# Two edits to an attention and mixture-of-experts kernel: the order and the queues of the first loads, and the place of one pair of copies

## The chip, the cores and the metric

The kernel runs on one core of a Trainium2 chip. The metric is the device time of one execution in microseconds (us). A core has five engines that run their own instruction streams in order and meet through semaphores: TensorE (PE; its weight loads are listed apart as PEld), VectorE (DVE), ScalarE (ACT), GpSimd (POOL) and SyncE (SP), which here issues nearly all loads and stores.

## The reference

Two layers, of which the second takes the first one's output. All arrays are fp32.

```python
# attention: B, H, S, D = 4, 8, 768, 64; 24 blocks of 32 tokens
mask = |block_i - block_j| <= 1, or either of them is block 0 or 23,
       or block_j is one of the 3 blocks drawn for block_i (sampled_blocks[24, 3])
attn = softmax(where(mask, q @ k.T / 8, -1e9)) @ v
# mixture of experts on x[3072, 512] (attn by token, heads side by side), 8 experts of 512 -> 1024 -> 512
logits = x @ w_gate + modality_bias[modality_id]
e_idx  = argmax(logits);  gate_w = softmax(logits)[e_idx]
out    = gate_w * (relu(x @ w1[e_idx]) @ w2[e_idx])
```

## The kernel before

**Attention.** The batches are worked in two halves of two. For each half, the first and the last block of queries see all keys ("dense" items); the other 22 blocks are taken two at a time, as 11 tiles per half, 22 in all, numbered g = 0 to 21 ("sparse" items). A tile's keys and values are gathered on chip from those it needs: block 0 and 23, the neighbours, and the drawn blocks.

- The dense keys `kd`, queries `qd` and values `vd` are loaded at the start (`dense_k`, `dense_q`, `dense_v`). `dense_k(0)` is three DMAs: the first part of the keys (blocks 0 to 15 and 16 to 23), then the second part.
- `blk_raw` holds the drawn blocks' numbers, sent to all partitions. POOL copies them to `rb_i` (L212, `block_ids`), and DVE makes from them the masks of the sparse tiles in small steps (`tables`, L242 to L287). Engines also read `rb_i` for the addresses of the drawn blocks.
- `share_k` (L465, L469, L481, on POOL) copies a tile's keys out of `kd` into one of two key buffers. `fetch_v` and `fetch_own` (L490 to L496, L520, on SP) load a tile's values from memory into one of two value buffers; `share_v` (L503, on POOL) copies two strips of 32 partitions that the last tile's buffer holds already. `share_v` also loads the numbers of a later tile's blocks into POOL's registers, as long as there are any left.
- A dense item's steps: S scores (L378), M maximum (L391 to L394, DVE), X exponential (L400, ACT), T transposes (L410), A copies (L417), W weighing with the values (L430, L432), O division. A sparse item's: S (L532), M masking and minimum (L540, DVE), X (L548, ACT), T (L557), A (L562), W with the strips that all queries of the tile share (`weigh_shared`, L579), V with the drawn ones (`weigh_own`, L588), O, then the gate (L595 to L608).

**Order.** The order of all instructions on every engine is written by hand. The beginning is the list `START`, in which `blk` is POOL's copy of the block list, `SP16` sixteen steps of DVE's tables, `S00` the first dense scores and `M00` the first maximum:

```python
blk SP16 S00 S01 M00 S02 M01 X00 T00 X01 M02 T01 M03 X02 A00 T02 X03 A01 T03 kl0 ...
```

After it a loop goes through ticks, one item per tick: each step of an item lags its scores by a fixed count (`LAG`), and loads and copies hang on (tick, place) pairs, counted from the last item of an earlier tile. `VS = (11, 7)` puts a tile's `share_v` 11 ticks behind the last item of the tile two before it, at place 7; `VL` and `VG` do the same for `fetch_v` and `fetch_own`. `EARLY = (3, 3)` steps, at place 3, a generator that prepares the first two groups of the experts.

**Experts.** Tokens are routed in groups of 256 rows of one expert. Finished rows go to memory (`x_d`, L1235), and a group's rows are gathered from there by POOL with an indirect DMA, two of 128 rows per group (`gather`, L735). Group 0's gather is issued while attention still runs, as soon as 16 of the 24 row tiles are written. PE turns the rows (`column`, L742), then come the layers: up (L753 to L755), relu, down (L768 to L770), each as three products of high and low parts, which ACT and DVE split (L721, L724); results go out by an indirect DMA (L789).

The program's tiles, DMAs and waits are set by the framework: a DMA of SP or ACT signals one of eight semaphores in turn.

Of the kernel before, what the change touches and what calls it, by code (L numbers as in the profile page):

```python
# [13 lines left out]
I32 = mybir.dt.int32  # L14
# [6 lines left out]
P = 128  # L21
# [18 lines left out]
NM = NB // 2 - 1  # L40
# [27 lines left out]
QP = (-2, 2)  # L68
VL = (8, 1)
VS = (11, 7)  # L70
VG = ((9, 6), (10, 3))

DENSE_IN = ((19, 14, 30), (49, 38, 44))
# [15 lines left out]
def attention_moe(ctx, tc, kD, qD, qH, v0, v1, blocks, modality, w_gate, bias, w1, w2, out):  # L89
    nc = tc.nc  # L90
# [28 lines left out]
    with ExitStack() as actx:  # L119
# [9 lines left out]
        def slot(n, dt=F32):  # L129
            return big.tile([P, 3 * 1024 + 2], dt, name="slot", tag=f"slot{n}", bufs=1)  # L130
# [8 lines left out]
        qd = {}  # L139
# [3 lines left out]
            nc.sync.dma_start(q_raw.rearrange("p n f -> p (n f)"), qH[half, m])  # L143
            return q_raw.rearrange("p n (u q) -> p u n q", q=32)

        def dense_q(half, u0=0, u1=8):
            if half not in qd:
                qd[half] = work.tile([P, HB * NPAIR, 64], F32, name="qd", bufs=1)
            nc.sync.dma_start(qd[half][:, u0:u1].rearrange("p u q -> p (u q)"), qD[half][:, 64 * u0:64 * u1])

        def dense_k(b, cs=(0, 1), js=None):
            if b not in kd:
                kd[b] = slot(KD_SLOT[b])[:, 0:3072].rearrange("p (c j f) -> p c j f", c=2, j=NB)
            for c in cs:
                for j0, j1 in js or (((0, 16), (16, 24)) if (b, c) == (0, 0) else ((0, 24),)):
                    nc.sync.dma_start(kd[b][:, c, j0:j1, :].rearrange("p j f -> p (j f)"), kD[b, :, c, j0 * 64:j1 * 64])
# [5 lines left out]
                nc.sync.dma_start(vd[b][:, t:t + n, :], vH[b // HB][t * P:(t + n) * P, b % HB].rearrange("(t p) f -> p t f", p=P))  # L162

        blk_raw = const.tile([P, NB * 3 * 2], I32, name="blk_raw")
        nc.sync.dma_start(blk_raw, blocks.bitcast(I32).rearrange("a b -> (a b)").partition_broadcast(P))
        dense_q(0, 0, 4)
        wg_raw = const.tile([P, NPAIR, E], F32, name="wg_raw")
        mod_raw = const.tile([P, NT, 2], I32, name="mod_raw")
        b_raw = const.tile([P, 2, E], F32, name="b_raw")

        dense_k(0)
        dense_q(0, 4, 8)
        dense_k(1, (0,))
        dense_v(0)
# [281 lines left out]
        def key_numbers(g):  # L456
            i = 2 * (g % NM) + 1
            picked[g] = nc.values_load_multi_w_load_instructions(
                rb_i[0:1, 3 * i:3 * i + 6], [ET.Pool], min_val=0, max_val=NB - 1, skip_runtime_bounds_check_because=NO_CHECK)[1]

        def share_k(m, half):
            i, g = 2 * m + 1, half * NM + m
            kg = kbuf[g % 2]
            if m:
                nc.gpsimd.tensor_scalar(kg[:, 3:5, :], kbuf[(g - 1) % 2][:, 7:9, :], 1.0, 1.0, ALU.mult, ALU.mult)  # L465

            def put(slots, blocks, bs):
                for b in bs:
                    nc.gpsimd.tensor_scalar(kg[:, slots, b * P:(b + 1) * P].rearrange("p s (c f) -> p c s f", c=2), kd[half * HB + b][:, :, blocks, :], 1.0, 1.0, ALU.mult, ALU.mult)  # L469

            if g not in picked:
                key_numbers(g)
            for bs in ((0,), (1,)) if g == 0 else (range(HB),):
                if m < 2:
                    put(slice(5, 7), slice(0, NB, NB - 1), bs)
                if m == 0:
                    put(slice(3, 5), slice(i - 1, i + 1), bs)
                put(slice(7, 9), slice(i + 1, i + 3), bs)
                for k, reg in enumerate(picked[g]):
                  for b in bs:  # L480
                    nc.gpsimd.tensor_copy(kg[:, k + k // 3 * 6, b * P:(b + 1) * P].rearrange("p (c f) -> p c f", c=2), kd[half * HB + b][:, :, bass.ds(reg, 1), :].rearrange("p c j f -> p c (j f)"))  # L481


        def fetch_v(m, half):
            i, g = 2 * m + 1, half * NM + m
            vg = vbuf[g % 2]
            vrow = vH[half].rearrange("(j s) b f -> s j (b f)", s=BLK)
            if m < 2:
                for n, j in ((0, 0), (1, NB - 1)):
                    nc.sync.dma_start(vg[32 + 32 * n:64 + 32 * n, 1, :], vrow[:, j, :])  # L490
            if m == 0:
                nc.sync.dma_start(vg[0:32, 1:3, :], vrow[:, i:i + 3:2, :])
                nc.sync.dma_start(vg[96:P, 0:2, :], vrow[:, i - 1:i + 2:2, :])
                return
            nc.sync.dma_start(vg[0:32, 2, :], vrow[:, i + 2, :])
            nc.sync.dma_start(vg[96:P, 1, :], vrow[:, i + 1, :])  # L496


        def share_v(m, half):
            g = half * NM + m  # L500
            new, old = vbuf[g % 2], vbuf[(g - 1) % 2]
            for r, c in ((slice(96, P), 0), (slice(0, 32), 1)):
                nc.gpsimd.tensor_scalar(new[r, c, :], old[r, c + 1, :], 1.0, 1.0, ALU.mult, ALU.mult)  # L503
            g = max(picked) + 1
            if g < 2 * NM:
                key_numbers(g)
# [8 lines left out]
        def fetch_own(m, half, n):  # L515
            i, g = 2 * m + 1, half * NM + m
            vg = vbuf[g % 2]
            vrow = vH[half].rearrange("(j s) b f -> s j (b f)", s=BLK)
            for k, reg in enumerate(own[g][3 * n:3 * n + 3]):
                nc.sync.dma_start(vg[32 * (k + n):32 * (k + n) + 32, 2 * n, :], vrow[:, bass.ds(reg, 1), :].rearrange("p j f -> p (j f)"))  # L520
# [676 lines left out]
        def side(t, f, place=7):  # L1197
            work_at.setdefault((t, place), []).append(f)
# [44 lines left out]
        def q_load(m, half):  # L1243
            qraw[m, half] = fetch_q(half, m)
            own_numbers(m, half)

        spares.append(tables())
        side(Q_IN, lambda: dense_q(1))
        for b in (2, 3):
            for t in range(6):  # L1250
# [5 lines left out]
        last = lambda g: at["s", g // NM, g % NM, 1, 1]  # L1256
        for g in range(2 * NM):
            half, m = divmod(g, NM)
            t = at["s", half, m, 0, 0]
            kl = lambda m=m, half=half: q_load(m, half)  # L1260
            qp = lambda m=m, half=half: share_k(m, half)
            vl = lambda m=m, half=half: fetch_v(m, half)
            vg = [lambda m=m, half=half, n=n: fetch_own(m, half, n) for n in range(2)]
            if g < 2:
                loads.update({f"kl{g}": kl, f"qp{g}": qp, f"vl{g}": vl, "vs1": lambda: share_v(1, 0), **{f"v{n}{g}": vg[n] for n in range(2)}})
                continue
            kt = last(g - 2) + KL[0]
            pt = max(kt, t + QP[0])
            vt = last(g - 2) + VL[0]
            side(kt, kl, KL[1])  # L1270
            side(pt, qp, QP[1])
            side(vt, vl, VL[1])
            if m:
                side(last(g - 2) + VS[0], lambda m=m, half=half: share_v(m, half), VS[1])
            for n in range(2):
                side(last(g - 2) + VG[n][0], vg[n], VG[n][1])

# [166 lines left out]
```

## Time and profile before

| what | value |
|---|---|
| median of 3 runs | 535.45 us (535.43 to 536.15) |
| the profiled execution | 536.03 us, span 534.3 us, mean granted PE clock 0.987 |
| PE busy | 514.9 us, 96% of the span |
| PEld, DVE, ACT, POOL busy | 82%, 71%, 63%, 40% |
| DMA | 119.44 MB, mean 224 GB/s |
| idle PE, ended by something | a few waits of at most 2.7 us each |

How to read it: the profiled execution is one run, its span goes from the first to the last instruction, and the device time has 1.7 us more around it. The engines' busy times are shares of that span. A line such as L503 is a line of the kernel's source; the same line stands for all tiles, so that a tile is told by its time. In a timeline, a row has the start, the duration, the engine, the line, the operation, what it writes and reads, and in brackets how long the engine stood idle before and what ended that. "issue" there means a wait for nothing that the profile shows. "SPq" is the queue side of an engine, which issues DMAs. Attention with its routing takes the first 232 us or so, the experts the rest.

### The profile page before, as it was taken

To read this page: it belongs to the slowest core of one execution; us is meant where nothing else is said; L and a number is where in the kernel's file an instruction comes from. 1 tells how busy PE (TensorE), PEld (TensorE's weight loads), DVE (VectorE), ACT (ScalarE), POOL (GpSimd) and SP (SyncE) were. 2 spreads that over 40 slices of the span, in tenths; PEclk is the share of its full clock that TensorE was granted. 3 is DMA by queue.
4 is the path that set the end of the run, shared out by engine and by line. 5 is a ranking of instruction groups with operands and counts; after the bars stand their busy time and mean duration, and the time that the engine had idled before them with its cause. 6 is when DMAs were issued, how large, how long until landed. Compare 5 with 4: busy or idle time off the path is not lost.

```text
span 534.3 us, 19017 instructions
## 1 busy us (share of the span) xinstructions
PE 514.9 (96%) x7298; PEld 436.1 (82%) x7298; DVE 377.2 (71%) x1139; ACT 335.2 (63%) x765; POOL 214.9 (40%) x451
## 2 busy tenths in 40 slices
PE   7999999998999999899999999999999999999995
PEld 5667776766778777788989898998989899898984
DVE  7995698683788999867997656556565655656553
ACT  4689877884988878835456554546555454655552
POOL 3577685574468884323155022030302203030213
PEclk9999999997999999899999999999999999999998
DMA  7995887898846798965888686676758677675840
GB/s 278 339 234 153 238 244 224 243 229 223 232 126 194 198 231 252 274 193 200 238 288 303 227 261 200 237 252 202 244 177 261 203 227 242 213 246 180 257 155 23
DMA packets 49443, 119.44 MB, mean 224 GB/s; under 512 B 7744, under 2 KB 8128, under 8 KB 49344
## 3 DMA queue, kind: packets, MB, share of 16 engines
q1 hardware_dynamic: 45248, 105.02, 64.5%
q0 software_dynamic: 4096, 13.12, 7.3%
q8 instruction: 59, 0.97, 0.8%
q14 instruction: 40, 0.33, 0.2%
HBM read 105.52 MB, written 12.86 MB: 222 GB/s over the span
## 4 chain that ended last, share of the span: by engine, by line
issue 40%; PE 39%; DVE 7%; DMA 6%; POOL 6%; SPq 2%; ACT 1%; POOLq 0%; DVEq 0%; ACTq 0%
PE bank L557 7%; PE bank L532 6%; PE bank L579 4%; PE bank L588 4%; POOL slot L735 3%; DMA out<-slot,si 2%; DMA slot<-kD 2%; PE bank L605 2%; POOL out L789 2%; PE bank L595 2%; DVE y L540 2%; PE bank L753 1%; PE bank L769 1%; PE bank L770 1%; PE bank L768 1%
## 5 line engine op out<-in xcount | busy, mean ns | idle before, releaser
L724 DVE TENSOR_TENSOR slot<-slot 128x1024 fp32r<-128x1024 f32 x99 | 123.1, 1248 | 89.3 <-ACT slot L721 87.5
L721 ACT CAST slot<-slot 128x1024 fp32r<-128x1024 f32 x104 | 108.1, 1048 | 102.1 <-PE bank L754 52.1
L753 PE MATMUL bank<-slot 128*128 128x256 f32 x384 | 108.4, 282 | 0.0
L755 PE MATMUL bank<-slot 128*128 128x256 f32 x384 | 107.8, 281 | 0.0
L754 PE MATMUL bank<-slot 128*128 128x256 f32 x384 | 107.7, 280 | 0.0
L789 POOL DMA_INDIRECT out<-slot,si x20 | 25.4, 1270 | 178.6 <-ACT slot L785 175.6
L548 ACT ACTIVATE a<-y,mn 128x256 f32<-128x256 f32 x176 | 88.7, 511 | 7.7 <-DVE mn L540 7.6
L768 PE MATMUL bank<-slot 128*128 128x512 f32 x192 | 76.6, 399 | 0.0
L769 PE MATMUL bank<-slot 128*128 128x512 f32 x192 | 75.9, 395 | 0.0
L770 PE MATMUL bank<-slot 128*128 128x512 f32 x192 | 75.8, 395 | 0.0
L753 PEld LDWEIGHTS bank<-slot 128*128 128x128 f32 x384 | 72.3, 188 | 0.6
L754 PEld LDWEIGHTS bank<-slot 128*128 128x128 f32 x384 | 72.1, 188 | 0.4
L755 PEld LDWEIGHTS bank<-slot 128*128 128x128 f32 x384 | 72.2, 188 | 0.0
L540 DVE CUSTOM_DVE_ANT_1 y<-bank,smask 128x256 f32<-128x256 f32 x176 | 66.3, 416 | 0.6 <-PE bank L532 0.2
L481 POOL COPY slot<-slot 128x128 f32 x264 | 63.9, 294 | 0.0
L562 ACT COPY at<-bank 128x512 f32<-128x512 f32 x88 | 50.6, 576 | 12.8 <-PE bank L557 12.7
L557 PE MATMUL bank<-ident,a 128*128 128x128 f32 x352 | 52.8, 284 | 0.6 <-ACT a L400 0.5
L503 POOL TENSOR_SCALAR slot<-slot 32x1024 f32<-32x1024 f32 x40 | 41.9, 1048 | 28.0 <-PE bank L588 10.2
L532 PE MATMUL bank<-slot,q_raw 64*32 64x256 f32 x1408 | 48.8, 382 | 1.1 <-DMA q_raw<-qH 0.7
L770 PEld LDWEIGHTS bank<-slot 128*128 128x128 f32 x192 | 36.1, 188 | 8.4
L557 PEld LDWEIGHTS bank<-ident,a 128*128 128x128 f32 x352 | 38.9, 142 | 4.7 <-ACT a L548 0.8
L769 PEld LDWEIGHTS bank<-slot 128*128 128x128 f32 x192 | 36.1, 188 | 7.8 <-DVE slot L724 0.4
(302 smaller groups left out, 855.4 us busy)
## 6 DMA issues: line engine op xcount, KB each, us to landing
slot<-w SPq DMA_DIRECT2D x100, 512.0 KB, 4.0
slot<-v SPq DMA_DIRECT2D x180, 128.0 KB, 4.0
x_d<-xr SPq DMA_DIRECT2D x22, 256.5 KB, 5.3
q_raw<-qH SPq DMA_DIRECT2D x22, 256.0 KB, 4.8
slot<-v SPq DMA_DIRECT2D x16, 256.0 KB, 4.9
slot<-kD SPq DMA_DIRECT2D x13, 256.0 KB, 4.2
slot<-v SPq DMA_DIRECT2D x4, 768.0 KB, 11.9
slot<-w SPq DMA_DIRECT2D x10, 256.0 KB, 5.1
```

Source lines behind the costliest of these rows:

```text
L532: nc.tensor.matmul(sp[u][32 * pr:32 * pr + 32, b * 256:(b + 1) * 256], lhsT=q[r, b * NPAIR + pr, n, :], rhs=kv[r, s0:s0 + 8, b, pr, :], st ...
L540: nc.vector.tensor_tensor_reduce(y[:, u, :].rearrange("p (s f) -> p s f", s=8), sp[u][:, b * 256:(b + 1) * 256].rearrange("p (s f) -> p s ...
L548: nc.scalar.activation(a[:, u, :], y[:, u, :], AF.Exp, bias=mn[:, u:u + 1], scale=-1.0, accum_out=total[:, u:u + 1])
L557: nc.tensor.transpose(tp[:, k:k + P], a[:, u, c * P:(c + 1) * P], ident)
L721: nc.scalar.copy(h, s)
L724: (eng or (nc.gpsimd if n in POOL_SPLITS else nc.vector)).tensor_tensor(l, s, h.bitcast(F32), ALU.subtract)
L753: nc.tensor.matmul(o, lhsT=h[:, fs], rhs=xh[g % 2][:, c, :], start=c == 0 and f % 2 == 0, stop=False)
L754: nc.tensor.matmul(o, lhsT=h[:, fs], rhs=xl[g % 2][:, c, :], start=False, stop=False)
L755: nc.tensor.matmul(o, lhsT=l[:, fs], rhs=xh[g % 2][:, c, :], start=False, stop=c == 3 and f % 2 == 1)
L768: nc.tensor.matmul(o, lhsT=hh[0][:, f, ts_], rhs=h[:, fs], start=f == 0, stop=False)
L769: nc.tensor.matmul(o, lhsT=hh[0][:, f, ts_], rhs=l[:, fs], start=False, stop=False)
L770: nc.tensor.matmul(o, lhsT=hl[f // 4][:, f % 4, ts_], rhs=h[:, fs], start=False, stop=f == 7)
```

## The change

Two edits.

1. The first loads. Before, SP issued in this order: block list, first half of the queries, the keys of batch 0 (three DMAs), second half of the queries, and so on. After, SP begins with the first two DMAs of the keys; the first half of the queries and then the block list are issued by ACT, ahead of its first instruction; SP goes on with the keys' second part and the rest as before. `dense_q` takes the issuing engine as an argument.
2. The copies of `share_v` for g = 20, the last tile but one, move from 11 to 8 ticks behind the last item of tile 18, at the same place 7. In POOL's order they now stand ahead of the two indirect DMAs of group 0's gather (L735) instead of behind them. All other tiles keep their place.

```diff
 VS = (11, 7)
+VS_SOON = (8, 7)
...
-        def dense_q(half, u0=0, u1=8):
+        def dense_q(half, u0=0, u1=8, eng=nc.sync):
             if half not in qd:
                 qd[half] = work.tile([P, HB * NPAIR, 64], F32, name="qd", bufs=1)
-            nc.sync.dma_start(qd[half][:, u0:u1].rearrange("p u q -> p (u q)"), qD[half][:, 64 * u0:64 * u1])
+            eng.dma_start(qd[half][:, u0:u1].rearrange("p u q -> p (u q)"), qD[half][:, 64 * u0:64 * u1])
...
         blk_raw = const.tile([P, NB * 3 * 2], I32, name="blk_raw")
-        nc.sync.dma_start(blk_raw, blocks.bitcast(I32).rearrange("a b -> (a b)").partition_broadcast(P))
-        dense_q(0, 0, 4)
...
-        dense_k(0)
+        dense_q(0, 0, 4, nc.scalar)
+        dense_k(0, (0,))
+        nc.scalar.dma_start(blk_raw, blocks.bitcast(I32).rearrange("a b -> (a b)").partition_broadcast(P))
+        dense_k(0, (1,))
         dense_q(0, 4, 8)
         dense_k(1, (0,))
         dense_v(0)
...
             if m:
-                side(last(g - 2) + VS[0], lambda m=m, half=half: share_v(m, half), VS[1])
+                vs = VS_SOON if g == 2 * NM - 2 else VS
+                side(last(g - 2) + vs[0], lambda m=m, half=half: share_v(m, half), vs[1])
```

## The prediction

> **What bounds the kernel now.** I read the page first (busy shares), then busy time by stretch, then the waits of TensorE (PE), then the timeline at the two places that the change touches.
>
> ```profile
> PE 514.9 (96%) x7298; PEld 436.1 (82%) x7298; DVE 377.2 (71%) x1139; ACT 335.2 (63%) x765; POOL 214.9 (40%) x451
> 6.00:24.00 18.00, 15.18 (x224) 9.69 (x229) 16.48 (x59) 10.59 (x33) 7.55 (x25) 1.00 1.01 361
> 24.00:38.00 14.00, 13.49 (x306) 9.64 (x294) 13.22 (x59) 11.35 (x39) 10.60 (x32) 1.00 0.94 228
> 38.00:205.00 167.00, 160.71 (x4137) 124.26 (x4136) 128.43 (x611) 137.90 (x449) 116.15 (x321) 0.98 0.77 214
> ```
>
> The page's row gives shares of the span, the others one stretch each: length, busy time of PE, PEld, DVE, ACT, POOL, then granted clock, DMA share, GB/s. From 24 us on PE is busy all but 0.5 us of 14 and 6.3 of 167: a microsecond lost or won ahead of 24 goes through to the end. Before 24 PE idles 2.8 us while DVE has 16.48 of 18 and DMA is full. So part one of the change (the first loads) is judged by what DVE and DMA do before 24 us, part two (the copies of tile 20, the last but one) by what PE waits for around 216 us.
>
> **Part one, the start.** The timeline (start, duration, engine, line, what ended the idle time), then from the waits of DVE between 4 and 25 us the one that is not in the timeline above it, and from the list of DMA issues the size and the time from issue to landing:
>
> ```profile
> 0.81 0.40 SPq L165 DMA_DIRECT2D blk_raw<-blocks  x1
> 0.81 1.28 ACT L214 ACT_TABLE_LOAD   x1 [0.81 <-PEq L1437]
> 1.26 0.42 SPq L149 DMA_DIRECT2D qd<-qD  x1
> 1.73 1.37 SPq L156 DMA_DIRECT2D slot<-kD  x3
> 3.99 0.24 POOL L212 COPY rb_i<-blk_raw 128x72 int32<-128x72 int32 x1 [1.99 <-DMA blk_raw<-blocks]
> 4.26 0.20 DVE L242 CAST rb<-rb_i 128x72 f32<-128x72 int32 x1 [0.43 <-POOL rb_i L212]
> 6.88 0.41 PEld L378 LDWEIGHTS bank<-slot,qd 64*64 64x64 f32 x8 [0.45 <-DMA slot<-kD]
> 7.85 0.19 DVE L268 TENSOR_TENSOR rm<-rm,t 128x24 f32<-128x24 f32 x1
> 7.96 0.69 DVE L391 TENSOR_REDUCE nm<-bank 128x1 f32<-128x512 f32 x1
> 9.10 1.52 PE L378 MATMUL bank<-slot,qd 64*64 64x512 f32 x16 [1.35 <-DMA slot<-kD]
> 9.32 0.69 ACT L400 ACTIVATE a<-bank,nb__263 128x512 f32<-128x512 f32 x1 [7.02 <-DVE nb__263 L394]
> 24.87 0.64 PEld L410 LDWEIGHTS bank<-ident,a 128*128 128x128 f32 x6 [0.41 <-ACT a L400]
> DVE nm L391 <- PE bank L378: 0.4, 1, 0.4
> blk_raw<-blocks SPq DMA_DIRECT2D x1, 72.0 KB, 3.1
> ```
>
> Removed from SP's queue: two issues, 0.81 to 1.73, so the keys and all that follows them start 0.92 us earlier. Added to ACT's: the same two, ahead of the table load (1.28); that then ends at 3.0, and the first exponential is at 9.32: nothing, and 6 us of cover.
>
> What do earlier keys buy? PE's 0.45 at 6.88 and 1.35 at 9.10. But the first maximum on DVE (L391 at 7.96) stands in DVE's order behind the first sixteen steps of the block tables (L242 at 4.26 to L268, ended 8.04) and starts the moment they are done. DVE's only other wait up to 25 us is the 0.4 in the last row but one, at the fifth maximum; the first four follow without a gap, they feed the exponentials, and those PE's transposes up to 24.87 (released by ACT). So PE's waits for keys are covered by DVE: I price the earlier keys at 0. If DVE's cover went they would bring 0.45 to 0.92.
>
> The tables hang on the block list: landing, POOL's copy at 3.99, DVE at 4.26. The list loses its place as first load: it becomes ACT's second issue, 1.26 instead of 0.81. With the same 3.1 us it lands 0.45 later: the lower bound. But now it moves beside keys that were issued at 0.81. No row shows a start like this; the nearest is the gather, a second queue beside SP's loads:
>
> ```profile
> GB/s 0 9 113 182 348 391 360 371 399 381 326 332 358 410 438 401 395 393 391 393 298 326 321 199 260 274 242 234 246 250 242 221 258 223 240 205 119 174 234 391
> DMA to landing us min/median/max: 3.4/5.8/7.7
> DMA to landing us min/median/max: 6.3/6.3/6.3
> ```
>
> The first row is DMA's rate in each of the first 40 us. The first landing row (shortest, median, longest) covers the gathers of the groups from the third on, the second the two of group 0, among SP's loads. A gather is 128 rows of 513 numbers, 257 KB; crowding costs it 6.3 - 3.4 = 2.9 us. Were the list hit like that, it would land at 1.26 + 6.3 = 7.6 instead of 3.9: +3.6, the upper bound. It has 72 KB, so I scale the 2.9 by 72/257 to 0.8, which is nearer to the lower end, and take 0.45 + 0.8 = +1.25 us for DVE's tables, the first maximum and PE at 24.87.
>
> The Trainium skill ("DMA: Bandwidth & Descriptors", Issuing engines are not separate DMA queues, and Queues, rings and completion order) says that the queues share the same 16 DMA engines, which change queue packet by packet, so a second issuer saves issue time alone. By that the list comes at the latest right behind the first keys, whose second piece released PE at 6.88 and would now be there by 5.96: at most +2.0 for the list, and at most +1.3 for the sum below. That no bandwidth is won agrees with the DMA share of 1.01 from 6 to 24 us.
>
> What gives some of it back: later, DVE's table steps run into POOL's copies, and PE has two waits.
>
> ```profile
> 29.27 2.16 POOL L503 TENSOR_SCALAR slot<-slot 32x1024 f32<-32x1024 f32 x2 [2.74 <-DMA slot<-v]
> 29.33 1.19 DVE L280 TENSOR_TENSOR btmp<-modf,b_raw 128x192 f32<-128x192 f32 x1
> 30.44 1.08 DVE L282 TENSOR_SCALAR nm<-modf 128x24 f32<-128x24 f32 x1
> 33.12 0.42 DVE L284 TENSOR_TENSOR btok<-nm,b_raw 128x192 f32<-128x192 f32 x1
> 36.76 1.10 PE L532 MATMUL bank<-slot,q_raw 64*32 64x256 f32 x32 [0.49 <-DVE xrd L451]
> 38.62 1.15 PE L579 MATMUL bank<-slot,at 128*64 128x64 f32 x30 [0.50 <-ACT at L562]
> ```
>
> L280 and L282 take 1.19 and 1.08 under POOL's two copies; L284, as large as L280, takes 0.42 outside them. POOL's copies wait for a DMA, which comes no later; with DVE 1.25 later the two meet less. PE can recover at most its own idle time there, 0.49 + 0.50. I take 0.75 of it. Part one: 1.25 - 0.75 = **+0.5 us**, bounds 0.45 - 0.99 = -0.5 and +3.6.
>
> **Part two, tile 20's copies.** POOL and PE around the first gather, and DVE where the copies will stand:
>
> ```profile
> 202.83 2.19 POOL L503 TENSOR_SCALAR slot<-slot 32x1024 f32<-32x1024 f32 x2
> 209.03 1.19 POOL L735 DMA_INDIRECT slot<-x_d,gi_e  x1 [4.01 <-DVE mn L540]
> 210.52 0.96 POOL L735 DMA_INDIRECT slot<-x_d,gi_e  x1 [0.30 <-issue]
> 217.02 4.54 POOL L503 TENSOR_SCALAR slot<-slot 32x1024 f32<-32x1024 f32 x4 [5.54 <-DMA slot<-x_d,gi_e]
> 207.15 1.21 PE L588 MATMUL bank<-slot,at 128*32 128x64 f32 x64
> 209.00 0.17 DVE L1017 TENSOR_SCALAR to<-to 128x2 f32<-128x2 f32 x1
> 218.07 0.43 PE L588 MATMUL bank<-slot,at 128*32 128x64 f32 x16 [1.83 <-issue]
> 219.97 1.96 PE L579 MATMUL bank<-slot,at 128*64 128x64 f32 x32
> 221.87 0.48 PE L742 MATMUL bank<-ident,slot 128*128 128x128 f32 x1
> 219.00:222.00 3.00, 3.00 (x54) 2.71 (x53) 3.00 (x13) 2.12 (x6) 2.41 (x3) 0.65 1.06 301
> 222.00:226.00 4.00, 4.00 (x95) 3.82 (x97) 2.95 (x13) 2.89 (x8) 0.00 (x0) 0.83 1.00 261
> ```
>
> The copies of tile 20 (first two of the four at 217.02) stand behind both gathers and wait 5.54 us for their landing. Their user, L579 at 219.97, starts without a wait: they were done at 217.02 + 2.19 = 219.2. PE itself was late: it stood 1.83 us at 216.25, in the middle of L588, for nothing that the profile shows. So the 5.54 us cost PE 0. Moved ahead of the gather, the copies wait for the last reader of their rows, L588 of tile 18 (ends 208.36), and run to 210.55. They issue no register loads (the numbers up to tile 21 are there) and no DMAs. Behind them queue the gathers: 210.6 instead of 209.03, landing by 210.6 + 1.5 + 6.3 = 218.4; their user, L742, is at 221.87: 3.5 us of cover, so 0. Tile 21's copies need L588's end at 218.5 anyway. DVE pays: L1017 and the step behind it fall under the two copies, some 0.8 us each by L280 and L282, and the maxima behind them come up to 1.6 later; what PE transposes next was made two items earlier, so I say 0, bound +1.0. Sum of part two: **0**, from -3.6 (next part) to +1.0.
>
> **Sum.** The profiled execution has 536.03 us (span 534.3), 0.58 above the median 535.45; +0.5 makes 536.5 of the one and 535.95 of the other. Some 0.2%, 1.07 us, is what a measurement here can tell from no change: I forecast none.
>
> **Rivals.** *A, faster.* The 1.83 us stall is a late load of PE's own instructions: DMA listed by window shows none between 214.4 and 215.5 and one (q8) after it:
>
> ```profile
> q1 hardware_dynamic: 150, 0.36, 107.6%
> q8 instruction: 1, 0.02, 5.4%
> ```
>
> The two rows are of 215.5 to 216.9: packets, MB and share of the 16 engines, q1 being SP's loads. The granted clock after it is 0.65 over 3 us and 0.83 over 4: 1.05 + 0.68 = 1.73 us lost. If the later gather clears the way, both go: 535.95 - 1.83 - 1.73 = 532.4, and then the early copies are needed. For: the gather's rows moved until just then. Against: SP's loads alone fill DMA after 216.
>
> *B, slower.* The list waits beside the keys as group 0's gather did (+3.6, less 0.75): 538.3. It decides from a landing at about 5.7 (+1.8, net more than 1.07). For: four loads of keys are then in flight. Against: 72 KB, and DMA moves 9 GB/s in the second microsecond and 113 in the third.
>
> *C, no effect:* the list lands 0.45 later and PE's idle time takes it up: 535.4.
>
> **How the numbers follow.** My forecast 0.32 and C 0.12, both within 0.2%; A, or part of it, 0.28; B 0.18; a stall of A's kind that is new or longer 0.10 (about 537.5). So faster 0.28, same 0.44, slower 0.28. The range 532.3 to 537.8 holds A and the near part of B and leaves out some 0.15. The forecast's own range is 534.9 to 536.5.
>
> **What would show it.** POOL's L212 near 5.2 and L391 near 9.2: right; at 4.0 and 8.0, part one costs nothing. PE's L410 of 24.87 near 26.1. L503 ahead of L735 and no wait for a gather; L742 unmoved against L579; a gap of PE at tile 19's L588 or none decides A. I am wrong if DVE does not hold the first maximum, or if the order of DMA moves PE's instruction loads.

## The result and the profile after

The changed kernel took 541.04 us (median of 14 runs, 536.82 to 547.03), the kernel before 536.06 in the same comparison (14 runs, 532.50 to 540.75). The ratio is 1.0089, 95% interval 1.0065 to 1.0114: slower by 4.8 us (3.5 to 6.1). I had forecast 535.95 with a range of 532.3 to 537.8.

The profiled execution of the changed kernel is the longest of its 14 (547.03 us, span 545.3, clock 0.987). So I read places and waits from it, not the total. First the page's row of busy times, then two stretches of busy time; there, after the length, come PE, PEld, DVE, ACT, POOL, then granted clock, DMA share, GB/s.

```profile
PE 517.5 (95%) x7298; PEld 437.3 (80%) x7298; DVE 379.1 (70%) x1139; ACT 335.5 (62%) x765; POOL 216.7 (40%) x451
```
```profile
6.00:24.00 18.00, 13.15 (x170) 8.66 (x167) 14.68 (x51) 8.61 (x27) 9.30 (x32) 0.91 1.01 369
24.00:38.00 14.00, 13.27 (x287) 9.64 (x288) 13.20 (x59) 11.38 (x39) 7.60 (x22) 1.00 0.82 218
```

Between 6 and 24 us PE lost 2.0 us of work (13.15 for 15.18) and DVE 1.8 (14.68 for 16.48); DMA is as full as before, and PE's granted clock is 0.91 instead of 1.00. The timeline of the start says why, and behind it stand DMA's rate in the first 6 us, in slices of 0.15 us, and the list of DMA issues (size, time from issue to landing):

```profile
0.80 1.34 SPq L157 DMA_DIRECT2D slot<-kD  x3
0.80 0.41 ACTq L150 DMA_DIRECT2D qd<-qD  x1
1.24 0.46 ACTq L172 DMA_DIRECT2D blk_raw<-blocks  x1
6.27 1.52 PE L380 MATMUL bank<-slot,qd 64*64 64x512 f32 x16
7.11 0.24 POOL L214 COPY rb_i<-blk_raw 128x72 int32<-128x72 int32 x1 [5.11 <-DMA blk_raw<-blocks]
7.38 0.20 DVE L244 CAST rb<-rb_i 128x72 f32<-128x72 int32 x1 [3.55 <-POOL rb_i L214]
9.06 1.52 PE L380 MATMUL bank<-slot,qd 64*64 64x512 f32 x16 [1.27 <-DMA slot<-kD]
11.40 0.20 DVE L270 TENSOR_TENSOR rm<-rm,t 128x24 f32<-128x24 f32 x1
11.53 0.68 DVE L393 TENSOR_REDUCE nm<-bank 128x1 f32<-128x512 f32 x1
12.89 0.69 ACT L402 ACTIVATE a<-bank,nb__263 128x512 f32<-128x512 f32 x1 [9.66 <-DVE nb__263 L396]
13.81 0.85 PE L412 MATMUL bank<-ident,a 128*128 128x128 f32 x6 [3.23 <-ACT a L402]
```
```profile
GB/s 0 0 0 0 0 0 0 0 0 0 0 0 164 191 137 55 82 34 123 198 348 362 294 464 512 362 273 458 410 330 390 405 300 227 204 95 33 87 12 117
...
slot<-kD SPq DMA_DIRECT2D x1, 512.0 KB, 4.3
slot<-kD SPq DMA_DIRECT2D x1, 256.0 KB, 5.2
qd<-qD ACTq DMA_DIRECT2D x1, 128.0 KB, 4.4
...
blk_raw<-blocks ACTq DMA_DIRECT2D x1, 72.0 KB, 5.8
```

(L214, L244, L393, L402, L412 are L212, L242, L391, L400, L410 of before.) The list takes 5.8 us from issue to landing, where it took 3.1. POOL's copy is at 7.11 instead of 3.99, DVE idles 3.55 us for it (0.43 before), the first maximum slides from 7.96 to 11.53, the first exponential from 9.32 to 12.89, and PE waits 3.23 us for that one. PE's 0.45 us wait for the first keys is gone and buys nothing. In the rate row the last 0.75 us run at 12 to 117 GB/s.

At the second edit's place, POOL, DVE, ACT and PE; then the issue of the gathers:

```profile
216.61 2.22 POOL L505 TENSOR_SCALAR slot<-slot 32x1024 f32<-32x1024 f32 x2 [6.01 <-DMA slot<-v]
219.01 1.18 POOL L737 DMA_INDIRECT slot<-x_d,gi_e  x1 [0.18 <-POOL slot L505]
220.49 1.91 POOL L737 DMA_INDIRECT slot<-x_d,gi_e  x1 [0.31 <-issue]
217.24 0.51 ACT L550 ACTIVATE a<-y,mn 128x256 f32<-128x256 f32 x1 [1.52 <-DVE mn L542]
217.95 0.88 DVE L1025 TENSOR_TENSOR si_e<-to,pad 128x2 int32<-128x2 f32 x1
224.28 0.43 PE L590 MATMUL bank<-slot,at 128*32 128x64 f32 x16 [1.28 <-issue]
229.30 0.98 PE L744 MATMUL bank<-ident,slot 128*128 128x128 f32 x7 [0.59 <-DMA slot<-x_d,gi_e]
239.48 0.72 PE L590 MATMUL bank<-slot,at 128*32 128x64 f32 x37 [2.70 <-DMA slot<-v]
```
```profile
slot<-x_d,gi_e POOLq DMA_INDIRECT x2, 8.4
```

(Here and in most kernels below, L505, L542, L550, L581, L590, L737, L744 and L1025 are L503, L540, L548, L579, L588, L735, L742 and L1023 of before.) The copies stand ahead of the gather, as meant, and wait for no gather. But the gathers now land 8.4 us after issue (6.3 before), and PE waits 0.59 us for the second of them. The 2.70 us of the last row are a wait for values of a later tile. It is there with the loads alone (2.04 us) and with the copies alone (1.87 us) too, so it can't be laid to the early copies.

### The profile page after: what moved, and what is told of

Same layout as the page of the kernel before. It is cut to its first block, busy times and chain, and to the rows that moved or that the text cites. A ratio compares the mean times of both kernels' runs of the same rounds, so it can differ in the third digit from the quotient of the medians.

```text
span 545.3 us, 19015 instructions
## 1 busy us (share of the span) xinstructions
PE 517.5 (95%) x7298; PEld 437.3 (80%) x7298; DVE 379.1 (70%) x1139; ACT 335.5 (62%) x765; POOL 216.7 (40%) x451
## 4 chain that ended last, share of the span: by engine, by line
issue 40%; PE 27%; DVE 14%; DMA 11%; POOL 5%; ACT 2%; SPq 1%; POOLq 0%; ACTq 0%; DVEq 0%
PE bank L534 5%; PE bank L559 5%; DMA slot<-v 4%; DMA out<-slot,si 3%; PE bank L590 3%; DVE y L542 3%; POOL slot L737 2%; PE bank L581 2%; PE bank L607 2%; POOL out L791 2%; PE bank L412 2%; DMA slot<-x_d,gi 2%; PE bank L380 1%; PE bank L434 1%; DVE slot L726 1%
## 5 line engine op out<-in xcount | busy, mean ns | idle before, releaser
L550 ACT ACTIVATE a<-y,mn 128x256 f32<-128x256 f32 x176 | 88.6, 510 | 10.0 <-DVE mn L542 9.9
L542 DVE CUSTOM_DVE_ANT_1 y<-bank,smask 128x256 f32<-128x256 f32 x176 | 66.4, 417 | 0.5
L505 POOL TENSOR_SCALAR slot<-slot 32x1024 f32<-32x1024 f32 x40 | 41.7, 1043 | 43.2 <-DMA slot<-v 13.9
```

The source lines that it names most:

```text
L542: nc.vector.tensor_tensor_reduce(y[:, u, :].rearrange("p (s f) -> p s f", s=8), sp[u][:, b * 256:(b + 1) * 256].rearrange("p (s f) -> p s ...
L550: nc.scalar.activation(a[:, u, :], y[:, u, :], AF.Exp, bias=mn[:, u:u + 1], scale=-1.0, accum_out=total[:, u:u + 1])
```

## The experiments

Each experiment's text of expectation stands as it was recorded. Times are ratios to the kernel before on the same chip. Besides them I use one reading of the trace: ACT's instructions are matched one by one with those of the kernel before, and the median difference of the 19 that start there between 33 and 40 us is the **shift** that the start leaves behind. Within the 19 it differs by at most 0.4 us, and nothing that happens later can disturb it. Equal starts differ in it by chance, though: the three kernels with the loads and the tables of before have 0, -0.21 and -0.40 (before, the copies alone, the copies made three times), the two with the changed loads +2.72 and +3.24. So I take differences up to 0.5 us for none.

**The loads alone.** Edit: the new loads, without `VS_SOON`.

> The changed loads alone, tile 20's copies back behind the gather. Theory L (the late block list costs the time: POOL's copy of it at 7.11 instead of 3.99 us, the first maximum at 11.53 instead of 7.96): the first maximum again near 11.5, and nearly the whole loss, +3.5 to +4.5 us over the kernel before. Theory P (the copies ahead of the gather cost the time, by a later gather at tile 20 and a later load for tile 21): the start is as late, but made up before 60 us, and the time is within 1 us of before. Theory F (only the places of PE's instruction loads moved): within 1.5 us of before, no steady sign.

Ratio 1.0060 (1.0031 to 1.0089), +3.2 us. POOL's copy at 7.05, first maximum 11.47, shift +2.72. Theory L holds for most of the loss; it had said +3.5 to +4.5.

**The copies alone.** Edit: `VS_SOON`, with the old loads.

> Tile 20's copies ahead of the gather alone, the loads as in the kernel before. Theory L: within 1 us of before. Theory P: +3 to +5 us, with a wait of PE for the gather at tile 20's L742 or for rows of v at tile 21. My prediction priced this part at 0, with bounds of -3.6 and +1.0.

Ratio 1.0016 (0.9983 to 1.0050). No loss that one comparison can tell from none. P as the whole cause falls.

**Where the list stands.** Two orders of the same loads, both without the copies:

```diff
-        dense_q(0, 0, 4, nc.scalar)
-        dense_k(0, (0,))
-        nc.scalar.dma_start(blk_raw, ...)
+        nc.scalar.dma_start(blk_raw, ...)      # second kernel: nc.sync
+        dense_q(0, 0, 4, nc.scalar)
+        dense_k(0, (0,))
         dense_k(0, (1,))
```

> As the changed loads alone, but the block list is ScalarE's first load and the queries its second. If the list is late because it stands behind the queries and the keys in the DMA engines (bytes ahead of it): it lands at 3.9 to 4.6 us, the first maximum is near 8.0 to 8.6, and the time within 1 us of before. If a second queue beside SyncE's is itself slow (theory of the queue): the list lands after 5.0 us all the same, and the loss stays above +2 us.

> As the changed loads alone, but the block list is SyncE's first load again; the queries stay on ScalarE's queue, and the keys come second, 0.45 us earlier than before. Theory L: list at 3.9, first maximum near 8.0, time within 0.7 us of before (a gain for the keys, if they are worth anything, of at most 0.45). Theory P or F: as for the changed loads alone.

As ACT's first load the list lands at 6.37: issued at 0.81, as before, and still 2.4 us later than there. Ratio 1.0030 (1.0001 to 1.0059), shift +1.63. Neither theory fits whole: the landing is behind 5.0 as by the theory of the queue, but the loss (+1.6 us) is less than the +2 that went with it. So it is not only the place behind the queries that delays the list: here the queries come behind it, and what is issued along with it are keys, from SP's queue. As SP's first load it lands at 5.36, not at the 3.9 that I expected, which is 1.4 us later than before. Two things differ there: 128 KB of queries are issued at the same moment from ACT's queue, and the first keys follow 0.45 us sooner. Which of them it is was not told apart. That costs the kernel nothing that can be measured: 0.9976 (0.9942 to 1.0011), shift +0.27.

**A list that is later still.** Edit: the list as SP's fourth load, behind the keys of batch 0's first two parts.

> The suspected cost made larger: as the changed loads alone, but the block list is SyncE's fourth load, behind all keys of the first two pairs. If the list's landing sets the start, it lands near 9.5 us (the third piece of keys landed at 9.0), the first maximum is near 14 us, the shift at 33 to 40 us grows from +2.7 to about +5, and the ratio from 1.006 to about 1.010. If the late list is not what costs the time, it stays near 1.006.

The timeline of this kernel's start:

```profile
9.82 0.24 POOL L214 COPY rb_i<-blk_raw 128x72 int32<-128x72 int32 x1 [7.82 <-DMA blk_raw<-blocks]
10.10 0.20 DVE L244 CAST rb<-rb_i 128x72 f32<-128x72 int32 x1 [6.27 <-POOL rb_i L214]
14.25 0.68 DVE L393 TENSOR_REDUCE nm<-bank 128x1 f32<-128x512 f32 x1
```

Ratio 1.0108 (1.0084 to 1.0132), +5.8 us, shift +5.87: the list's landing sets the start, as this experiment was to show. All in one table (us; the list as POOL starts to copy it):

| kernel | list | first exponential | shift | ratio |
|---|---|---|---|---|
| before | 3.99 | 9.32 | 0 | 1 |
| copies alone | 4.42 | 9.75 | -0.21 | 1.0016 |
| list first on SP | 5.41 | 10.74 | +0.27 | 0.9976 |
| list first on ACT | 6.43 | 12.23 | +1.63 | 1.0030 |
| loads alone | 7.05 | 12.82 | +2.72 | 1.0060 |
| the change | 7.11 | 12.89 | +3.24 | 1.0089 |
| list behind keys | 9.82 | 15.61 | +5.87 | 1.0108 |

The later list costs little up to about 5.4; from there to 9.82 it comes 4.4 us later and the shift grows by 5.6, some 1.3 us for each. Where the first microsecond goes and where the extra comes from is in the part on the prediction.

**Is it the first maximum, or DVE's time?** Edit, with the new loads alone: in the order written out by hand `blk SP16 S00 S01 M00 S02 M01 X00` becomes `blk S00 S01 M00 S02 M01 SP16 X00`, so that the table steps no longer hold the first two maxima.

> The changed loads alone, with the first sixteen steps of the block tables set behind the second maximum in DVE's order instead of ahead of the first. Theory H (the list only holds the head of the chain: first maximum, first exponential): the first maximum comes with its scores, near 7.7 to 8.0 us, the shift of ScalarE's work at 33 to 40 us falls from +2.7 to below +0.5, and the time is within 1 us of before. Theory D (DVE is full to 38 us, so what it idles before the list comes is lost, in whatever order the rest stands): the first maximum is early, but the third comes behind the tables at 12 to 13 us and the shift at 33 to 40 us stays +2 to +3.

```profile
6.77 0.69 DVE L393 TENSOR_REDUCE nm<-bank 128x1 f32<-128x512 f32 x1 [2.94 <-PE bank L380]
8.14 0.69 ACT L402 ACTIVATE a<-bank,nb__247 128x512 f32<-128x512 f32 x1 [4.91 <-DVE nb__247 L396]
9.13 0.19 DVE L244 CAST rb<-rb_i 128x72 f32<-128x72 int32 x1
13.19 0.68 DVE L393 TENSOR_REDUCE nm<-bank 128x1 f32<-128x512 f32 x1
15.38 2.42 PEld L412 LDWEIGHTS bank<-ident,a 128*128 128x128 f32 x12 [3.62 <-ACT a L402]
```

The first exponential comes at 8.14, earlier than in the kernel before, and nothing is gained: the third maximum comes at 13.19, PE's weight loads wait 3.62 us there, the shift is +3.94 and the ratio 1.0059 (1.0030 to 1.0088). Theory H falls. Theory D is right in kind, and a little short (it had said 12 to 13 us and +2 to +3): the steps take their some 4 us of DVE wherever they stand, and what DVE idled before is gone.

**The steps off DVE.** Edit: in `tables()` the first 22 steps on `nc.gpsimd` instead of `nc.vector`; once with the old loads, once with the new.

> The kernel before (its own loads and its own place of tile 20's copies) with the steps of the block tables on GpSimd, which waits for keys until 11 us, instead of DVE. Theory D: DVE gains the 3.8 us of the steps from 4.26 to 8.04; the first maximum comes with its scores near 7.5, and the work at 33 to 40 us is 1 to 3 us earlier: 0.2 to 0.6% faster. Theory H: only the head moves, from 7.96 to about 7.5: within 1 us of before. Against both: GpSimd's steps may take 0.3 us or more and its copies of keys at 11 us come later; then it is slower.

> The changed loads alone with the steps of the block tables on GpSimd: nothing of DVE's start hangs on the list. Theories D and H: the first maximum comes with its scores near 7.6 although the list lands at 7.0, and the shift at 33 to 40 us is within 0.5 us of that of the kernel with the old loads and the tables on GpSimd; what is left of the difference between the two is what the earlier keys bring (at most 0.45) less what GpSimd's later start costs. If the new loads cost time by themselves (rate of DMA, waits of PE for keys), the difference stays above 1 us.

The start of the second of them:

```profile
7.16 0.24 POOL L214 COPY rb_i<-blk_raw 128x72 int32<-128x72 int32 x1 [5.15 <-DMA blk_raw<-blocks]
7.33 0.69 DVE L393 TENSOR_REDUCE nm<-bank 128x1 f32<-128x512 f32 x1 [3.49 <-PE bank L380]
8.70 0.69 ACT L402 ACTIVATE a<-bank,nb__263 128x512 f32<-128x512 f32 x1 [5.47 <-DVE nb__263 L396]
9.10 1.52 PE L380 MATMUL bank<-slot,qd 64*64 64x512 f32 x16 [1.37 <-DMA slot<-kD]
```

The list is as late as in the changed kernel (7.16), and the loss is gone: ratio 0.9992 (0.9956 to 1.0028), shift -0.34. With the old loads: 0.9986 (0.9952 to 1.0021), shift +0.16. This shows the path: late list, tables on DVE, maxima. It also shows the limit of theory D: DVE freed of its steps gains no 1 to 3 us, since it then waits for PE's scores (3.49; 3.88 with the old loads) and PE for keys (1.37). And it bounds what the earlier keys bring where nothing covers them: 0.16 + 0.34 = 0.50 us by the shift of one execution each, no more than equal starts differ.

**The copies, where the start costs nothing.** Three kernels with the table steps on GpSimd: the whole change; a kernel meant to beat both (list first on SP); the same with the copies ahead.

> The whole change, with the steps of the block tables on GpSimd. If the list's hold on DVE is all that the change costs: within 1.5 us of before, the work at 33 to 40 us within 0.5 us of before's, as with the new loads and these tables without the copies (-0.34, ratio 0.9992). If the copies ahead of the gather cost by themselves what the difference of 1.0089 and 1.006 suggests: +1.5 us beside that kernel. If they gain what PE waited for them where they stood behind the gather (0, 1.3, 0, 2.7, 3.0, 1.1 and 0 us in seven profiled executions, mean 1.2): 1.2 us faster than that kernel.

> A kernel meant to beat both: list as SyncE's first load, keys second, queries on ScalarE, tables on GpSimd, copies behind the gather. The list lands near 5.3 and delays nothing; the keys come 0.45 us earlier than before. The head gives up its wait of DVE: the work at 33 to 40 us 0.3 to 1.0 us earlier, time 0 to 1 us below before; if earlier keys and a free DVE are worth nothing there, the ratio is 1.000 within its interval.

> As the kernel meant to beat both, with tile 20's copies ahead of the gather. Beside it, on the same chip, this gives what the copies are worth where the start costs nothing: 0 by the prediction, -1.2 us by the mean wait of PE for them, +1.5 us by the difference of the first two ratios.

Ratios 1.0025 (0.9994 to 1.0055), 0.9982 (0.9945 to 1.0018), 1.0012 (0.9975 to 1.0049); shifts -0.46, -0.46, -0.30. The kernel meant to beat both can't be told from the one before. Its keys did not come earlier, as I had expected: its first maximum waits for PE's scores until 8.16, in the kernel with the old loads and these tables until 7.72. There are now four pairs with and without the early copies: +0.16% (copies alone), 0.33% (1.0025 - 0.9992), 0.30% (1.0012 - 0.9982) and 0.29% (1.0089 - 1.0060). No pair is sure by itself (each is uncertain by 0.3 to 0.5%); their mean is +0.27%, 1.4 us, uncertain by 0.22%.

**The gather later still.** Edit: with the copies alone, tile 20's two copies each made three times.

> The copies alone (old loads), but each of tile 20's two copies ahead of the gather is made three times: the gather's issue is 4.4 us later still, nothing else changes. By my prediction the gather had 3.5 us to spare after the move: then PE waits some 1 us at L742's transposes (4.4 - 3.5), +1 us of the copies alone. If there is less to spare, as PE's waits of 0.2 and 0.6 for it in the changed kernel suggest: +3 to +4.4 us.

```profile
208.23 7.70 POOL L505 TENSOR_SCALAR slot<-slot 32x1024 f32<-32x1024 f32 x6 [5.99 <-PE bank L607]
216.11 1.18 POOL L737 DMA_INDIRECT slot<-x_d,gi_e  x1 [0.18 <-DVE gs L319]
222.78 0.45 PE L744 MATMUL bank<-ident,slot 128*128 128x128 f32 x1 [1.22 <-DMA slot<-x_d,gi_e]
224.50 1.76 PE L744 MATMUL bank<-ident,slot 128*128 128x128 f32 x7 [1.28 <-DMA slot<-x_d,gi_e]
```

Ratio 1.0064 (1.0029 to 1.0098), 2.6 us above the copies alone (1.0064 - 1.0016), a difference as uncertain as it is large. PE waits 1.22 + 1.28 = 2.50 us for the gathers, so a gather issued late enough does hold PE. How much time was to spare can't be read from it: the copies took 7.70 us where they take 2.17 with the copies alone, 5.5 more and not 4.4, these gathers landed 6.7 us after issue and not 8.3, and PE itself came later to its transposes, since it had waited 1.80 us for ACT just before. The kernel with the copies alone shows the spare time directly (the list of DMA issues gives the time to landing):

```profile
208.55 2.17 POOL L504 TENSOR_SCALAR slot<-slot 32x1024 f32<-32x1024 f32 x2 [3.95 <-PE bank L558]
212.38 0.96 POOL L736 DMA_INDIRECT slot<-x_d,gi_e  x1 [0.30 <-issue]
221.13 1.09 PE L743 MATMUL bank<-ident,slot 128*128 128x128 f32 x8
```
```profile
slot<-x_d,gi_e POOLq DMA_INDIRECT x2, 8.3
```

The second gather takes 8.8 us of these two (the first 7.8) and lands at 221.15; the transposes (L743) begin at 221.13, and the second of them, the first to need it, follows at 221.3. So some 0.15 us were to spare, where I had counted 3.5.

## Why the prediction was wrong

**The block list: the step that failed.** I took +1.25 us for its landing, by scaling the gather's crowding of 2.9 us with size (72 of 257 KB), and gave rival B, the list that waits like the gather, 0.18. It landed 3.1 us later, close to B's +3.6. The scaling with size had no row to stand on. What the runs varied is what is in flight with the list, and the delay follows that: as first load, with queries on the other queue, it came 1.4 us later, with the first keys on the other queue 2.4, behind the queries and beside the keys 3.1, behind three pieces of keys 5.8. The list's own size was the same in all of them, so that size plays no part is not shown. The nearest row was the gather's, and taken as it stood it would have been 0.5 us off.

The sentence on the Trainium skill ("DMA: Bandwidth & Descriptors", Issuing engines are not separate DMA queues) bore up better than my term: it says that transfers from several engines run on the same 16 DMA engines and interleave. The trace agrees: the list came soon behind the first two pieces of keys (the second, issued at 1.25, at 6.41; the list at 7.05). Worked from it, I had +2.0 at most. That fell 1.1 us short: 0.45 since I let the keys come by 5.96, a full 0.9 us earlier, where they won 0.4 (6.84 to 6.41), and 0.64 since the list landed that much behind them, in a stretch where DMA's rate sinks to 12 to 117 GB/s.

**The way from the list to PE: right, but for what the delay gathers on the way.** DVE holds the first maximum, and the tables hold DVE. Two things happen to the delay behind that. The median differences of ACT's start times, as for the shift, show both (us later than before):

| kernel | list | first exponential | 28 to 33 us | 33 to 40 us (the shift) |
|---|---|---|---|---|
| list first on SP | 1.42 | 1.42 | 1.36 | 0.27 |
| list first on ACT | 2.44 | 2.91 | 2.74 | 1.63 |
| loads alone | 3.06 | 3.50 | 3.60 | 2.72 |
| the change | 3.12 | 3.57 | 4.11 | 3.24 |
| list behind keys | 5.83 | 6.29 | 7.03 | 5.87 |

At the place that I had named, 0.87 to 1.16 us come back in each of them, whatever the delay; I took 0.75 and at most 0.99. The way I had named holds too: the two table steps that took 1.19 and 1.08 us under POOL's copies take 0.35 and 0.26 behind them in the changed kernel (first two rows). What I put at nothing is that the delay grows first, from 3.12 to 4.11 us in the changed kernel. The sixteen table steps, later, run into POOL's copies of keys (0.34 us for a step of 0.19, third row) and take 4.15 us instead of 3.70; and the fifth maximum waits 1.0 us for PE's scores, 0.4 before. This fits the table of landings: a list of 5.41 costs next to nothing, since about one microsecond comes back, and each later one costs somewhat more than it is late.

```profile
34.28 0.35 DVE L282 TENSOR_TENSOR btmp<-modf,b_raw 128x192 f32<-128x192 f32 x1
34.56 0.26 DVE L284 TENSOR_SCALAR nm<-modf 128x24 f32<-128x24 f32 x1
9.72 0.34 DVE L266 TENSOR_TENSOR t<-t 128x24 f32<-128x24 f32 x1
```

Put the measured +3.1 in place of +1.25 and my own sum gives 3.1 - 0.75 = +2.35 for part one; measured were, with the loads alone, +2.72 by shift and +3.2 by time. By the rule I had set for B, a landing after 5.7 decides: it was 7.0.

**The earlier keys: right under DVE's cover.** PE's wait for them went and nothing was gained. Without the cover I had said 0.45 to 0.92; the 0.50 measured is within the chance of single executions, and the ratios (0.9986 and 0.9992) show no gain. Nor did ACT's later table load cost anything: the first exponential waits for DVE.

**Part two: the cover was too large, and DVE's share was dropped.** I priced it at 0; it probably costs 1.4 us (0.27%, uncertain by 0.22%). Three sub-steps can be judged.
- The gather's landing. The issue came where I had put it (second gather at 212.38 with the copies alone; I had 212.1). But I let it take 6.3 us to land, from one execution, and it took 8.8. So 0.15 us were to spare with the copies alone and less than nothing in the changed kernel, where PE waits 0.59 us. What lengthens the landing was not isolated: the median of the two gathers is 8.3 to 8.7 in four of the five kernels with early copies and 6.7 in the fifth (the copies made three times); with the copies at their old place it is 6.1 to 7.4 in four kernels and 8.6 in a fifth, as far as the traces have it.
- DVE. I saw that two steps would stall some 0.8 us each and set that at 0, with 1.0 as bound. In each of the five kernels with early copies, one small step, not two, stretches to 0.88 to 1.03 us (L1025 above). ACT's wait for DVE's maximum at this place is 1.36 to 1.89 us in all five and 0.75 to 0.90 in the nine without, the one before among them (row below). In three of the five a wait of 0.70 to 0.85 us of L443 for a DMA of finished rows goes into it. That is 0.75 us more on the mean, half of the 1.4, and it is a wait of ACT; how much of it reaches PE was not isolated.
- The benefit. "The 5.54 us wait of POOL costs PE 0" was true only of the one execution I had: PE itself stood 1.83 us there. In five of the nine kernels with the old place, PE did wait for the copies, 0.5 to 3.0 us, as in the kernel with the list first on SP (row below). With early copies none of the five kernels waits there; by the four pairs, these copies still cost more than they gain.

The first line is from the timeline of the kernel before, the second from the waits (total, times, longest) of the kernel with the list first on SP, between 203 and 232 us:

```profile
210.89 0.51 ACT L548 ACTIVATE a<-y,mn 128x256 f32<-128x256 f32 x1 [0.75 <-DVE mn L540]
```
```profile
PE bank L581 <- POOL slot L505: 2.7, 1, 2.7
```

**Rival A** (a gain of 3.6 us by ending PE's stall at L588) did not come: the stall is there in the changed kernel (1.28 us, in L590 at 224.28), and between 0.83 and 1.56 us in seven more of the kernels above, early copies or not; in the one with the list behind keys it is 4.59 us.

**Sum.** Loads +3.2, copies +1.4: 4.6 of the measured 4.8 us. One of the four pairs behind the 1.4 holds the changed kernel itself; the other three alone give 1.4 as well (0.26%). What the loads cost is sure and their way to PE is shown; what the copies cost is probable, and its way is argued.

## What to carry to other kernels

The first small load of this kernel was cheap with nothing in flight ahead of it; issued from a second queue beside large loads it came in with them, small as it is. Before moving a load, ask what stands behind its landing in the consumers' own order, and read the cost of crowding from a transfer in the same kernel that was crowded; scale it only if a row shows how it scales. A cover read from one execution may be an accident of it, above all where the waiting engine is itself late for no visible reason.

## What was not expected of the hardware

- The first load of the first queue isn't safe from a second queue either: the list, first on SP at 0.80, landed at 5.28 and 5.36 with 128 KB from ACT's queue issued beside it and the keys 0.45 us sooner behind it, and at 3.93 to 4.37 without (three executions).
- PE's stalls that end by nothing visible move between executions of nearly the same program: the kernel before has 2.65 us at 121.60, the one with the loads alone 2.14 us at 105.41 and 0.76 at 124.50, the changed one 1.86 us at 109.51. They may account for part of the spread of single runs (532.5 to 540.75 us for the kernel before); with one trace of each kernel that isn't shown, and what sets them was not tried. The Trainium skill ("Runtime: NRT & Kernel Launch", Instruction fetch mechanics) calls the cost of fetching the next block of instructions mostly hidden; if these stalls are such fetches, which no run here isolates, it isn't hidden in this kernel.
